# Attention values in fp32 matmuls, means moved between engines, and expert rows fetched by plain loads

## The chip, the cores and the metric

The kernel runs on one NeuronCore of a Trainium2 chip. The metric is the device time of one execution in microseconds (us). A core has five engines that work side by side, each through its own queue of instructions: PE (TensorE, the matrix unit; its weight loads are listed as PEld), DVE (VectorE), ACT (ScalarE), POOL (GpSimd) and SP (SyncE, here only an issuer of DMA transfers). POOL issues DMAs too, above all the indirect ones, whose row addresses come from a table. PE writes its results to PSUM[...]; DVE and ACT read them from there. A loaded tile lies in SBUF, the large on-chip memory.

## The reference

For 8 batches of 8 heads (576 positions, head size 64) two attentions are added, and their sum goes through a mixture of 8 experts in which each row visits one expert:

```python
q_d = q.reshape(B, H, Sd, 4, D).mean(axis=3)      # likewise k_d, v_d: means of 4 rows
out_d = sm_attn(q_d, k_d, v_d)                    # softmax attention, 144 x 144
out_up = np.repeat(out_d, 4, axis=2)
mask = np.abs(pos[:, None] - pos[None, :]) < 4    # local band, 7 wide
out_local = softmax(where(mask, scale * q @ k.T, -1e9)) @ v
x = (out_up + out_local)                          # as [4608 rows, 512]

e_idx = argmax(x @ w_gate)                        # one of 8 experts for each row
eom = sigmoid(x @ w_output_gate)
for e in range(8):
    out[rows of e] = gate_w * eom[:, e] * (relu(x_e @ w1[e]) @ w2[e])   # 512 -> 1024 -> 512
```

## The kernel before

The attention is done in 32 units, each of two heads of one batch. A list of tasks with an engine, a planned cost and a priority is put in order when the program is built, and each engine runs its tasks in that order. One unit is this:

```python
def cast(u, i):      # POOL: q and k to fp16
def v_high(u):       # ACT: upper half of v in fp16 (v scaled by VS = 1024)
    nc.scalar.activation(d["vh"][:, :, 0:D], d["vf"], AF.Copy, scale=VS)
def v_low(u):        # DVE: the rest, v*VS - high, in fp16
    nc.vector.scalar_tensor_tensor(d["vl"], in0=d["vf"], scalar=VS, in1=d["vh"][:, :, 0:D], ...)
def turn(u):         # PE: q and k turned, and their means of four by a 0.25-matrix pm
    for i in range(2):
        for m in range(6):
            nc.tensor.matmul(tf[:, i, S // 2:S // 2 + SD], lhsT=t16[:, m, :], rhs=pm[:, m, :], ...)
        for m in range(6):
            nc.tensor.transpose(tf[...][:, 96 * m:96 * m + 96], t16[:, m, :], id16[0:96, 0:96])
def turned(u):       # ACT: both out of PSUM (qkT: 1152 columns, qkd: 288 columns)
def v_means(u):      # PE: means of v's four rows, out of the two halves
    for w in range(NW):                                        # NW = 10 windows of rows
        for i, m in enumerate((d["vh"], d["vl"])):
            for h in range(2):
                nc.tensor.matmul(pd[:, h, c:c + D], lhsT=pv[r, w, :], rhs=m[r, w, 0:D], ...)
def vd_high(u):      # ACT
def vd_low(u):       # DVE
def scores(u):       # PE
    for g in range(2):                                         # the band's mask, 504 columns
        nc.tensor.matmul(ps[:, g, 0:NH], lhsT=id16, rhs=mk[:, g, :], ...)
    for h, r in hs:                                            # means: 128 of 144 keys
        mm(ps[:, h, 0:SD], kd[r, 0:128], qd[r])
    ...                                                        # 20 of 64x57 or 64x60: the band
    ...                                                        # means: the last 16 keys
def e_high(u):       # ACT: exp twice, once to fp16 and once in place in fp32
    nc.scalar.activation(d["eh"], ps, AF.Exp, scale=scale)
    nc.scalar.activation(ps, ps, AF.Exp, scale=scale)
def e_low(u):        # DVE: the rest in fp16
def values(u):       # PE: (high, high), (high, low), (low, high) for each product
    ...              # 60 + 12 + 12 matmuls of 64 or 65 columns
def norm(u):         # DVE: reciprocal of the sums, two products
```

After each fourth unit a batch's 5 tiles of 128 rows are finished (`upsample`, `x_sum`, `x_high`, `x_low`, `x_turn`, `logits`), gated in groups (`pick`, `ranks`, `gate_sums`, `rows`), and written row by row to a table in HBM with one region for each expert (`scatter`, 40 indirect DMAs). Then come the experts, 5 tiles of 128 rows each; for the first two experts 3 tiles are done early, when only six batches are in the table.

```python
def gather(e, j):    # POOL, 40 times: 128 rows of expert e by an index table
    nc.gpsimd.indirect_dma_start(out=ex[e]["xg"][:, j, :], in_=xs_dram.ap(),
        in_offset=bass.IndirectOffsetOnAxis(ap=posg[...][:, e, j:j + 1], axis=0), ...)
def rows_out(e, js): # DVE: the output rows; slots past the expert's count get a row out of bounds
    nc.vector.tensor_tensor(o[...], d["xg"][..., Dm // 2 + 1], none_i[i][...], op=ALU.add)
def g_turn(e, js):   # PE transposes; g_turned: DVE copies them out
def up(e, part, fs): # PE: 4 x 8 matmuls of 384 and of 256 columns against w1
def relu(...)        # ACT and DVE
def down(e, ...):    # PE: 8 matmuls of 512 columns for each tile against w2
def weigh(e, j):     # ACT: times the row's weight
def put(e, j):       # POOL, 40 times: 128 rows to the output by index
```

The weights of an expert come by four DMAs that POOL issues (`load_part`); there is room for three experts' weights at a time.

Of the kernel before, what the change touches and what calls it, by code (L numbers as in the profile page):

```python
# [19 lines left out]
KW = [57 * w - 1 for w in range(10)]  # L20
NW = 10
NB = 5
# [13 lines left out]
def kernel(  # L36
# [22 lines left out]
    VS = 1024.0  # L59
    GS = 1024.0  # L60
    XS = 4.0 * VS
# [13 lines left out]
    NH = SD + NL + NK  # L75
    LC = [SD + Q0[w] - NL * (w // 5) for w in range(NW)]
    TC = SD + NL
    mk = cst.tile([128, 2, NH], F16)
    nc.vector.memset(mk, 32.0)
    band = cst.tile([64, 2, 64], F16)  # L80
    pv = cst.tile([128, NW, 128], F16)
    nc.vector.memset(pv, 0.0)
    pb = cst.tile([64, NW, 17], F16)
# [5 lines left out]
    def make_band():  # L89


        nc.gpsimd.memset(band, 32.0)
        select(band, 4, [[0, 2], [1, 64]], -1, -8192.0)
        select(band, 2, [[0, 2], [-1, 64]], 1, -8192.0)
        select(band[:, 0], -1, [[0, 64]], 1, -8192.0)

    def make_mask(h):
        r = slice(64 * h, 64 * h + 64)
        copy = nc.scalar.copy if h else nc.vector.tensor_copy
        for g in range(2):  # L100
            x = band[:, 1, 3:60]
            c = SD + 60 * (1 - g)
            copy(mk[r, g, c:c + 228].rearrange("p (w c) -> p w c", w=4), _ap(x, [x.ap[0], [0, 4], x.ap[1]]))
        copy(mk[r, 0, SD:SD + 60], band[:, 0, 0:60])
        copy(mk[r, 1, SD + 228:SD + 288], band[:, 1, 3:63])

    def make_means():
# [3 lines left out]
        select(pb[:, 0:NW - 1], -1, [[1, NW - 1], [-4, 17]], 1)  # L111
        select(pb[:, 0:NW - 1], 4, [[-1, NW - 1], [4, 17]], -1)
        select(pb[:, 0:NW - 1], 60, [[0, NW - 1], [0, 17]], -1)
        select(pb[:, 1:NW - 1], -4, [[0, NW - 2], [0, 17]], 1)
        select(pb[:, NW - 1], 0, [[-4, 17]], 1)
        select(pb[:, NW - 1], 3, [[4, 17]], -1)

    def spread_means(h):
        r = slice(64 * h, 64 * h + 64)
        copy = nc.scalar.copy if h else nc.vector.tensor_copy  # L120
        x = pv[r, 0, 0:17]
        copy(_ap(x, [x.ap[0], [142, NW - 2], x.ap[1]]), pb[:, 0:NW - 2])
        copy(pv[r, NW - 2, 112:128], pb[:, NW - 2, 0:16])
        for c in (0, 32):
            copy(pv[r, NW - 1, c:c + 16], pb[:, NW - 1, 0:16])

    pm = cst.tile([96, 6, SD], F16)

    def make_pm():

        nc.gpsimd.memset(pm, 0.25)
        select(pm, 0, [[1, 6], [-4, SD]], 6)
        select(pm, 3, [[-1, 6], [4, SD]], -6)
# [22 lines left out]
    slot_i = cst.tile([128, E, CAPJ], I32)  # L156
    slot_f = cst.tile([128, E, CAPJ], F32)
    reg_i = cst.tile([128, E, CAPJ], I32)
    reg_f = cst.tile([128, E, CAPJ], F32)
# [3 lines left out]
    def make_gate():  # L163
# [14 lines left out]

        nc.gpsimd.iota(slot_i, pattern=[[0, E], [128, CAPJ]], base=0, channel_multiplier=1)
        nc.gpsimd.iota(reg_i, pattern=[[-REG, E], [128, CAPJ]], base=E * REG, channel_multiplier=1)  # L180
# [8 lines left out]
    def gate_consts():  # L189
        for x in w9_s:  # L190
            nc.vector.tensor_copy(x[:, :, E], past)
        for o, x in ((rev, rev_i), (slot_f, slot_i), (reg_f, reg_i)):
            nc.vector.tensor_copy(o, x)
# [5 lines left out]
    vh_s, vdh_s, xh_s = [], [], []  # L199
    for i in range(4):  # L200
        t_vh = cst.tile([128, NW, 66], F16, tag=f"vh{i}")
        nc.vector.memset(t_vh[:, :, 64:66], 0.25)
        vh_s.append(t_vh)
        t_vd = cst.tile([128, 2, 2, 66], F16, tag=f"vd{i}")
        nc.vector.memset(t_vd[:, :, :, 64:66], 0.25)
        vdh_s.append(t_vd)
# [3 lines left out]
    nc.vector.memset(cum, 0.0)  # L210

    posg = [cst.tile([128, E, CAPJ], I32, tag=f"posg{i}", name=f"posg{i}") for i in range(2)]
    none_i = [cst.tile([128, E, CAPJ], I32, tag=f"none{i}", name=f"none{i}") for i in range(2)]
    cnts = [cst.tile([128, E], F32, tag=f"cnts{i}", name=f"cnts{i}") for i in range(2)]
# [38 lines left out]
    def load_v(u):  # L253
        b, hp = u // NP, u % NP
        st.setdefault(u, {})["vf"] = vf = sbA.tile([128, NW, D], F32, tag="vf", name="vf", bufs=4)
        for h in range(2):
            s, r = v[b, 2 * hp + h], slice(64 * h, 64 * h + 64)
            if u == 0 and h == 0:

                nc.vector.memset(vf[0:1, 0, :], 0.0)  # L260
                nc.sync.dma_start(vf[1:64, 0, :], s[0:63, :])
                nc.sync.dma_start(vf[r, 1:NW, :], _ap(s, [[D, 64], [57 * D, NW - 1], [1, D]], KW[1] * D))
            else:
                nc.sync.dma_start(vf[r], _ap(s, [[D, 64], [57 * D, NW], [1, D]], -D))
# [5 lines left out]

    def v_high(u):
        d = st[u]
        d["vh"] = vh_s[u % 4]
        nc.scalar.activation(d["vh"][:, :, 0:D], d["vf"], AF.Copy, scale=VS)  # L274

    def v_low(u):
        d = st[u]
        d["vl"] = sbA.tile([128, NW, D], F16, tag="vl", name="vl", bufs=4)
        nc.vector.scalar_tensor_tensor(d["vl"], in0=d["vf"], scalar=VS, in1=d["vh"][:, :, 0:D],  # L279
                                       op0=ALU.mult, op1=ALU.subtract)  # L280

    def turn(u):
# [3 lines left out]
        for i in range(2):  # L286
            t16 = d["s16", i].rearrange("p m h d -> p m (h d)")
            for m in range(6):
                nc.tensor.matmul(tf[:, i, S // 2:S // 2 + SD], lhsT=t16[:, m, :], rhs=pm[:, m, :],  # L289
                                 start=(m == 0), stop=(m == 5), skip_group_check=True)  # L290
            for m in range(6):
                nc.tensor.transpose(tf[:, i, :].bitcast(F16)[:, 96 * m:96 * m + 96], t16[:, m, :], id16[0:96, 0:96])  # L292

    def turned(u):

        d = st[u]
        d["qkT"] = sbA.tile([128, 2 * S], F16, tag="qkT", name="qkT", bufs=3)
# [658 lines left out]
```

The softmax here doesn't subtract the row's maximum and nothing guards it: scores larger than these inputs give would overflow.

## Time and profile before

| | before |
|---|---|
| median of 3 runs | 520.38 us (519.46 to 521.83) |
| span of the profiled run | 519.3 us |
| PE busy | 415.0 us, 80% |
| DVE busy | 247.3 us, 48% |
| ACT busy | 244.6 us, 47% |
| POOL busy | 280.7 us, 54% |
| HBM read and written | 68.23 MB and 15.77 MB |

Busy time of an engine is the time in which at least one of its instructions ran. Matmuls run in a pipeline, so their records overlap, and a mean of 200 ns for a small matmul does not say that each takes 200 ns of PE: the distance between two starts does. The page cuts the span into 40 equal slices and gives each engine's busy share in tenths. A group line gives the program line, the engine, the operation, the tile written and those read, the shape, the count, then busy time and mean duration, and then the idle time of the engine just ahead of these instructions and what ended it. In a table of windows each row is a stretch of the span with the busy time of each engine, the clock granted to PE as a share of full speed, and the busy share of the DMA engines. The attention's matmuls end at 299 us of the span, the experts' first matmul starts at 323 us, and the last one ends at about 505 us.

### The profile page before, as it was taken

The page shows a single profiled execution, that of the slowest core. Times are in us where ns is not written, and L with a number is a line of the kernel's source. Part 1 is how long each engine was busy: PE and PEld are TensorE (multiplying, and loading weights), DVE is VectorE, ACT ScalarE, POOL GpSimd, SP SyncE. Part 2 cuts the span into 40 slices and gives each one's busy share as a digit, 9 for nine tenths or more (in the row PEclk, how much of TensorE's full clock was granted, in tenths as well). Part 3 has the DMA queues.
Part 4 walks back from the last instruction along what each step waited for, and adds up shares of the span by engine and source line. Part 5 has one row for each costly group of instructions (what it writes and reads, how often), then busy time and mean ns, then how long its engine had stood idle before and what let it go on. Part 6 is the DMA issues. An engine that isn't in the chain of part 4 may idle for free.

```text
span 519.3 us, 17157 instructions
## 1 busy us (share of the span) xinstructions
PE 415.0 (80%) x7567; PEld 291.3 (56%) x7567; DVE 247.3 (48%) x494; ACT 244.6 (47%) x403; POOL 280.7 (54%) x315
## 2 busy tenths in 40 slices
PE   4866996979978869899969566977689759889990
PEld 3645684666756757675946434535455435456540
DVE  5436975656757747756658474412232012322200
ACT  4646784557747557766647332312223232333340
POOL 8724754525866815948426545576786524572231
PEclk9878898588979797976889755998989899999996
DMA  9999649465455595461450101233579994594121
GB/s 193 216 190 204 148 112 166 123 114 114 132 155 145 131 214 131 136 156 47 70 97 31 57 20 50 69 120 103 127 159 212 208 218 96 138 193 120 62 92 39
DMA packets 76285, 66.34 MB, mean 128 GB/s; under 512 B 46962, under 2 KB 67507, under 8 KB 76200
## 3 DMA queue, kind: packets, MB, share of 16 engines
q0 software_dynamic: 19840, 35.74, 30.7%
q1 hardware_dynamic: 56360, 29.40, 26.2%
q8 instruction: 61, 1.00, 0.8%
q14 instruction: 24, 0.20, 0.1%
HBM read 68.23 MB, written 15.77 MB: 162 GB/s over the span
## 4 chain that ended last, share of the span: by engine, by line
PE 58%; issue 17%; DVE 7%; DMA 6%; POOL 5%; another core or an unknown queue 2%; ACT 2%; POOLq 0%; DVEq 0%
PE pu L636 8%; PE tqk L289 7%; PE ps L336 5%; PE us L430 5%; PE pd L313 5%; PE po L385 4%; PE py L659 4%; PE tqk L292 4%; PE ps L338 3%; PE po L391 3%; DMA w1sb<-in_moe_w_dram 3%; PE tp L445 2%; PE po L401 2%; PE lg L465 2%
## 5 line engine op out<-in xcount | busy, mean ns | idle before, releaser
L269 POOL CAST qk<-qk 96x768 f16<-96x768 f32 x64 | 55.7, 882 | 76.6 <-issue 35.1
L636 PE MATMUL pu<-xgT,w1sb 128*128 128x384 f16 (+1 forms) x512 | 80.2, 315 | 19.2 <-DVE xgT L619 9.5
L636 PEld LDWEIGHTS <-w1sb 128*128 128x128 f16 x512 | 52.4, 103 | 46.0 <-issue 25.0
L671 POOL DMA_INDIRECT out_dram<-y,oi x40 | 40.3, 1006 | 49.7 <-ACT y L667 42.0
L659 PE MATMUL py<-w2sb,hs 128*128 128x512 f16 x272 | 61.6, 379 | 0.0
L667 ACT ACTIVATE y<-py,xh 128x512 f32<-128x512 f32 x40 | 25.6, 684 | 74.3 <-PE py L659 34.8
L651 DVE TENSOR_SCALAR hs<-pu 128x256 f16<-128x256 f32 x56 | 23.3, 423 | 67.1 <-ACT hs L649 40.4
L289 PE MATMUL tqk<-pm,qk 96*128 96x144 f16 x384 | 44.7, 264 | 13.1 <-POOL qk L269 6.2
L551 POOL DMA_INDIRECT hx_xs<-xh,pos x40 | 41.7, 1043 | 19.7 <-issue 8.4
L440 POOL TENSOR_TENSOR t_xl<-xo,xh 128x512 f16<-128x512 f32 x38 | 45.6, 1215 | 10.6 <-ACT xh L437 10.2
L587 POOL DMA_INDIRECT xh<-hx_xs,posg x40 | 40.7, 1017 | 17.8 <-issue 10.5
L300 ACT COPY qkT<-tqk 128x1152 f16<-128x1152 f16 x32 | 35.8, 1118 | 22.4 <-PE tqk L292 22.4
L649 ACT ACTIVATE hs<-pu 128x384 f16<-128x384 f32 (+1 forms) x56 | 26.1, 475 | 42.7 <-PE pu L636 34.4
L289 PEld LDWEIGHTS <-qk 96*128 96x128 f16 x384 | 31.7, 115 | 18.6 <-issue 7.4
L659 PEld LDWEIGHTS <-hs 128*128 128x128 f16 x272 | 26.2, 98 | 28.4
L279 DVE SCALAR_TENSOR_TENSOR vl<-vf,t_vh 128x640 f16<-128x640 f32 x32 | 39.9, 1249 | 3.0 <-ACT t_vh L274 3.0
L360 DVE TENSOR_TENSOR el<-ps,eh 128x1008 f16<-128x1008 f32 x32 | 38.3, 1198 | 4.3 <-ACT ps L355 4.3
L354 ACT ACTIVATE eh<-ps 128x1008 f16<-128x1008 f32 x32 | 32.5, 1016 | 13.1 <-PE ps L336 12.6
L313 PE MATMUL pd<-vl,pv 64*128 64x64 f16 x640 | 29.1, 200 | 11.8 <-issue 11.7
L413 DVE TENSOR_TENSOR xo<-po,rs 128x448 f32<-128x448 f32 x64 | 37.0, 619 | 1.5
L292 PE MATMUL tqk<-id,qk 96*128 96x96 f16 x384 | 34.2, 236 | 4.0 <-issue 4.0
L423 POOL TENSOR_TENSOR xdl<-xo,xdh 72x512 f16<-72x512 f32 x15 | 18.9, 1273 | 33.1 <-ACT xdh L418 33.1
(144 smaller groups left out, 896.4 us busy)
## 6 DMA issues: line engine op xcount, KB each, us to landing
vf<-in_v_dram SPq DMA_DIRECT2D x63, 160.0 KB, 7.6
qk<-in_q_dram SPq DMA_DIRECT2D x32, 288.0 KB
qk<-in_k_dram SPq DMA_DIRECT2D x32, 288.0 KB, 4.6
w1sb<-in_moe_w_dram POOLq DMA_DIRECT2D x16, 512.0 KB
w2sb<-in_moe_w_dram POOLq DMA_DIRECT2D x16, 512.0 KB
hx_xs<-xh,pos POOLq DMA_INDIRECT x40
xh<-hx_xs,posg POOLq DMA_INDIRECT x40
out_dram<-y,oi POOLq DMA_INDIRECT x40
```

Source lines behind the costliest of these rows:

```text
L269: nc.gpsimd.tensor_copy(t16.rearrange("p m h d -> p h m d"), d["f", i])
L279: nc.vector.scalar_tensor_tensor(d["vl"], in0=d["vf"], scalar=VS, in1=d["vh"][:, :, 0:D], op0=ALU.mult, op1=ALU.subtract)
L289: nc.tensor.matmul(tf[:, i, S // 2:S // 2 + SD], lhsT=t16[:, m, :], rhs=pm[:, m, :], start=(m == 0), stop=(m == 5), skip_group_check=True)
L292: nc.tensor.transpose(tf[:, i, :].bitcast(F16)[:, 96 * m:96 * m + 96], t16[:, m, :], id16[0:96, 0:96])
L313: nc.tensor.matmul(pd[:, h, c:c + D], lhsT=pv[r, w, :], rhs=m[r, w, 0:D], start=(w == 0 and i == 0), stop=(w >= NW - 2 and i == 1), skip_g ...
L360: nc.vector.tensor_tensor(d["el"], d["ps"][:, :, 0:NH], d["eh"], op=ALU.subtract)
L440: (nc.vector if b == B - 1 and t % 2 else nc.gpsimd).tensor_tensor(t_xl[:, t], xo_s[b][:, t, :], xh_s[b % 4][:, t, 0:Dm], op=ALU.subtract)
L551: ins = nc.gpsimd.indirect_dma_start(out=xs_dram.ap(), out_offset=bass.IndirectOffsetOnAxis(ap=gs[n]["pos"][:, c:c + 1], axis=0), in_=xh_s ...
L587: nc.gpsimd.indirect_dma_start(out=ex[e]["xg"][:, j, :], out_offset=None, in_=xs_dram.ap(), in_offset=bass.IndirectOffsetOnAxis(ap=posg[0 ...
L636: nc.tensor.matmul(ps[:, i, 0:x.shape[2]], lhsT=wts[e][0][:, c, 128 * f:128 * f + 128], rhs=x[:, c, :], start=(c == 0), stop=(c == 3))
L659: nc.tensor.matmul(ps[:, i, :], lhsT=d["hs"][:, f, c:c + 128], rhs=wts[e][1][:, f, :], start=(f == 0), stop=(f == NG - 1))
L671: ins = nc.gpsimd.indirect_dma_start(out=out, out_offset=bass.IndirectOffsetOnAxis(ap=d["oj", j], axis=0), in_=d.pop(("y", j)), in_offset= ...
```

## The change

It does three things, and orders the tasks anew.

1. **No halves.** v and the exponentials stay in fp32, and each product of the values is one fp32 matmul. The steps that made the halves go. The ones' column that gives the sums is 1/4096 in v's tile.
2. **Means.** v's means are fp32 matmuls with 32 weight columns that write 32 rows of PSUM each; the means of q and k (as sums of four; the exponential's scale is divided by 16) are a reduction on DVE over the turned q and k, and no longer matmuls. The keys' means are scored in four pieces of 32 rows, and the mask covers only the band's 288 columns.
3. **Plain loads.** The first 640 rows of each expert's region are filled ahead with empty rows whose output row is out of bounds. The experts' rows then come by one plain load for a pass (10 in all, issued by SP), the index tables and the correction of output rows go, and `put` takes its rows straight out of what was loaded.

```diff
-    def v_high(u): ...
-    def v_low(u): ...
     def turn(u):
...
-                nc.tensor.matmul(tf[:, i, S // 2:S // 2 + SD], lhsT=t16[:, m, :], rhs=pm[:, m, :],
-                                 start=(m == 0), stop=(m == 5), skip_group_check=True)
-            for m in range(6):
                 nc.tensor.transpose(tf[:, i, :].bitcast(F16)[:, 96 * m:96 * m + 96], t16[:, m, :], id16[0:96, 0:96])
...
+    def qk_means(u):
+        nc.vector.tensor_reduce(d["qkd"], d["qkT"].rearrange("x (n r) -> x n r", r=4), axis=AX.X, op=ALU.add)
...
     def v_means(u):
         for w in range(NW):
-            c = D * (w == NW - 1)
-            for i, m in enumerate((d["vh"], d["vl"])):
-                for h in range(2):
-                    nc.tensor.matmul(pd[:, h, c:c + D], lhsT=pv[r, w, :], rhs=m[r, w, 0:D], ...)
+            for h in range(2):
+                j, c = (w // 2, 0) if w < 8 else (2 * h + 1, D)
+                nc.tensor.matmul(pd[32 * j:32 * j + 32, h, c:c + D], lhsT=pv[64 * h:64 * h + 64, w, :],
+                                 rhs=d["v"][64 * h:64 * h + 64, w, 0:D], start=(w % 2 == 0), stop=(w % 2 == 1), ...)
-    def vd_high(u): ...
-    def vd_low(u): ...
+    def vd_out(u):                                  # ACT: three copies out of PSUM
...
     def scores(u):
-            nc.tensor.matmul(ps[:, g, 0:NH], lhsT=id16, rhs=mk[:, g, :], ...)
-        for h, r in hs:
-            mm(ps[:, h, 0:SD], kd[r, 0:128], qd[r])
+            nc.tensor.matmul(ps[:, g, 0:NL], lhsT=id16, rhs=mk[:, g, :], ...)
+        for j in range(4):
+            for h, r in hs:
+                mm(ps[32 * j:32 * j + 32, h, MC:NH], kd[r, MW[2 * j]:MW[2 * j] + 32], qd[r])
...
-        nc.scalar.activation(d["eh"], ps, AF.Exp, scale=scale)
-        nc.scalar.activation(ps, ps, AF.Exp, scale=scale)
-    def e_low(u): ...
+        d["e"] = e = sbA.tile([128, 2, NH], F32, tag="e", name="e")
+        nc.scalar.activation(e[:, :, TC:NH], d["ps"][:, :, TC:NH], AF.Exp, scale=scale / 16.0)
+        nc.scalar.activation(e[:, :, 0:TC], d["ps"][:, :, 0:TC], AF.Exp, scale=scale)
     def values(u):                                  # 20 + 4 + 4 fp32 matmuls of 65 columns
+                    nc.tensor.matmul(po[h][64 * a:64 * a + 64, t, :], lhsT=e[r, w // 5, LC[w]:LC[w] + 64],
+                                     rhs=t_v[r, w, 0:65], start=(t == 0), stop=False, skip_group_check=True)
...
     def norm(u):                                    # DVE: two reciprocals and three products, the means' rows apart
...
+    def prefill(e):                                 # SP, 8 times
+        nc.sync.dma_start(xs_dram.ap()[r:r + 128 * CAPJ, :].rearrange("(p j) d -> p (j d)", p=128), ...)
-    def gather(e, j): ...
-    def rows_out(e, js): ...
+    def fetch(e, part):                             # SP, 10 times
+        nc.sync.dma_start(ex[e]["xg"][:, j0:j1, :].rearrange("p j d -> p (j d)"),
+                          xs_dram.ap()[r:r + 128 * (j1 - j0), :].rearrange("(p j) d -> p (j d)", p=128))
...
-    LEAN = {"band": 0.1, "cast": -1.2, "eh": -2.15, ...}       # shifts of the tasks' priorities
+    LEAN = {"ahead": 67.55, "band": -52.05, "cast": -27.9, ...}
...
-                task(("scat", x, t), "POOL", 1.35, ..., [("rows", b)], scatter, n, x, t, ...)
+                task(("scat", x, t), "POOL", 1.35, ..., [("rows", b)] + [("fill", e) for e in range(E)], scatter, n, x, t, ...)
```

## The prediction

> **What bounds the kernel now.** I read the slices first, then a table of windows, then the chain that ended last, then groups and the timelines of single engines.
>
> ```profile
> PE   4866996979978869899969566977689759889990
> PEclk9878898588979797976889755998989899999996
> DMA  9999649465455595461450101233579994594121
> PE 58%; issue 17%; DVE 7%; DMA 6%; POOL 5%; another core or an unknown queue 2%; ACT 2%; POOLq 0%; DVEq 0%
> ```
>
> A slice is 13 us. PE is the fullest engine in nearly every slice and holds 58% of the chain; no other engine has over 7%. DMA is full only at the start and around the experts' weights. The windows split the span into three stages:
>
> ```profile
> 100.00:200.00 100.00, 83.90 (x2219) 66.79 (x2216) 64.01 (x115) 60.79 (x96) 53.25 (x54) 0.84 0.64 143
> 200.00:290.00 90.00, 79.25 (x2157) 60.62 (x2156) 60.33 (x110) 57.81 (x89) 54.59 (x55) 0.87 0.40 91
> 290.00:320.00 30.00, 17.03 (x244) 11.72 (x244) 15.09 (x43) 8.52 (x16) 13.06 (x13) 0.54 0.13 42
> 320.00:353.00 33.00, 26.23 (x174) 14.15 (x172) 12.16 (x40) 7.09 (x16) 20.57 (x21) 0.91 0.27 87
> 353.00:400.00 47.00, 39.48 (x269) 25.76 (x269) 12.78 (x32) 14.16 (x30) 34.37 (x36) 0.93 0.68 153
> ```
>
> The columns are PE, PEld, DVE, ACT, POOL, clock, DMA share, GB/s. In the attention (to 299 us) PE is busy 84 to 88%, DVE and ACT about 64%, so PE bounds it, with short waits between. From 290 to 353 us, the last batches' gating and the table's last rows, PE is busy 43 of 63 us. Then the experts: in 353 to 519 us I add the windows to 132 us of PE in 166. The holes in PE there have names in PE's timeline and in the waits:
>
> ```profile
> 353.40 5.32 PE L636 MATMUL pu<-xgT,w1sb 128*128 128x256 f16 x32 [4.01 <-DVE xgT L619]
> 377.40 7.11 PE L636 MATMUL pu<-xgT,w1sb 128*128 128x256 f16 x39 [4.02 <-DVE xgT L619]
> 420.05 0.61 PE L608 MATMUL gtp<-id,xh 128*128 128x128 f16 x8 [3.64 <-DVE xgT L619]
> DVE oi L599 <- DMA out_dram<-y,oi: 23.6, 5, 7.3
> ```
>
> PE waits for turned rows (xgT), and DVE, which turns them out, stands behind the correction of output rows (oi), which waits for an earlier output transfer. All holes over 0.2 us from 353 to 466 us add up to 24 us.
>
> **What the skill says.** The Trainium skill's page "FP8 and Floating Point Precision", section TensorE Precision Notes, says that a true fp32 product is four passes through the array. The kernel before has no fp32 matmul, so no trace here shows it yet. "TensorEngine Tiling (Array Packing)", Key Properties, says that tiles work independently, weight loads included. The trace agrees for fp16: in the timeline at 126 us four 64x64 matmuls of 65 columns take one step, and the next four start 30 to 40 ns later. "VectorE: DVE Perf Modes", section on the perf-mode tier table, gives a reduction no faster mode for 16-bit data; the trace has only short reductions (264 ns for 80 fp16 elements), which can't tell. "TensorE: Matmul & The Clock Gate", Part 1, says an idle PE falls to half its clock. The trace agrees: at 119.8 us such steps are 55 ns apart, and the window with most idle PE has a clock of 0.54.
>
> **The change part by part.** In 100 to 200 us there are 132 mean matmuls of line 289, 12 for a unit: 11 units, so a unit takes 9.1 us and 7.6 us of PE.
>
> ```profile
> L289 PE MATMUL tqk<-pm,qk 96*128 96x144 f16 x384 | 44.7, 264 | 13.1 <-POOL qk L269 6.2 <-DVE xo L413 3.9 <-issue 3.0
> L279 DVE SCALAR_TENSOR_TENSOR vl<-vf,t_vh 128x640 f16<-128x640 f32 x32 | 39.9, 1249 | 3.0 <-ACT t_vh L274 3.0
> L360 DVE TENSOR_TENSOR el<-ps,eh 128x1008 f16<-128x1008 f32 x32 | 38.3, 1198 | 4.3 <-ACT ps L355 4.3
> L354 ACT ACTIVATE eh<-ps 128x1008 f16<-128x1008 f32 x32 | 32.5, 1016 | 13.1 <-PE ps L336 12.6 <-PE us L430 0.5
> L587 POOL DMA_INDIRECT xh<-hx_xs,posg x40 | 40.7, 1017 | 17.8 <-issue 10.5 <-DMA hx_xs<-xh,pos 2.4 <-DVE xh L547 2.4
> ```
>
> PE, one unit at full clock. A column costs 0.42 ns (16 output matmuls of 512 columns in 3.62 us, the last one's 0.38 taken off: 0.216 us each).
> - Means of q and k: in the timeline six matmuls of 144 columns span 0.55 us, one of them 0.23, so 0.065 us a step; 12 of them: -0.78.
> - Mask: 504 to 288 columns, twice: 432 x 0.42 ns = -0.18.
> - Keys' means in 8 pieces instead of 2, partly side by side: +0.1.
> - Values: before, 84 matmuls from 125.85 to 127.97 us less a hole of 0.47: 1.65 us. After, with four passes of 65 x 0.42 = 27 ns: five rounds of four tiles side by side 0.55; four full-width ones 0.44; two pairs 0.22; 0.2 for the pipeline's end: 1.4. Weight loads that don't hide add perhaps 0.2: counted as 1.6, so -0.05.
> - v's means: 0.77 us before (the chain has 0.76 at 133 us); after, 10 pairs x 4 x 27 ns = 1.08 if the column tiles don't overlap, about half if they do. Counted 0.9: +0.13.
>
> Sum -0.78, and over the clock of 0.84, -0.9 us of 7.6. If PE stays 84% busy, a unit takes 8.0 instead of 9.1 us, 34 us in 32 units. I count 26, because a new step now stands in each unit's path (DVE's reduction of 1152 elements; by DVE's 1198 ns for 1008, some 1.35 us) and because more idle PE may lower the clock.
>
> ACT, one unit: gone are 0.74 + 0.41 + 2 x 1.02 + 0.37 = 3.55 us; the rows of 256 and 1008 elements give 0.85 ns an element and about 0.16 us fixed, so the new exponentials (432 and 576) cost 1.17 and the three copies 0.7: -1.7 us. DVE: gone are 1.25 + 1.20 + 0.42 = 2.87; the reduction costs 1.35, the longer norm 0.3: -1.2 us. Both lie beside PE; they shorten the time that a unit's scores hold PSUM (two exponentials and a subtraction, 3.2 us, become 1.2) and so fill some of PE's short holes.
>
> POOL: 40 gathers of 1.02 us and 0.3 between go, 53 us of its queue. Six stand between the last rows' steps (306 to 332 us), and five from 344.4 to 350.7 us ahead of the 4.0 us hole at 353. One load replaces each set: I count -8 us for 300 to 353 us. In the expert stage, of the 24 us of holes those that end on xgT or come from oi should mostly go, those that wait for weights should not: -13 us.
>
> SP: 8 fills of 128 x 5160 bytes, 5.3 MB; at the 200 GB/s of the page's fullest slices some 26 us of DMA time. In the built program they come behind the loads of the first ten units, where DMA is about half busy: 0.
>
> Sum: 26 + 8 + 13 = 47, so 520.4 - 47 = 473; I say 474 us.
>
> **The rivals.** (1) fp32 matmuls don't run side by side, or load their weights in the open. Then 48 of them at 108 ns are 5.2 us where I count 2.5, 2.7 us more in each unit, 86 us in all: 474 + 86 = 560. Against it: fp16 tiles, which load weights just as often, do overlap; for it: nothing in the trace has fp32. (2) DVE's reduction or DMA takes PE's place. DVE would be 51 of 100 us, ACT 43, so no engine is near; but with fills DMA rises from 187 us of the first 290 (shares of the windows times their lengths) to some 213 of 265. Then the attention gains only 10 us: about 490. (3) The experts are held by weights: the five last experts' 21 MB need 105 us at 200 GB/s, and the slices at 390 to 430 us already show 208 to 218. Then 13 becomes 5: about 482. (4) All holes in PE close: the attention gains 34 and the rest 30: about 455.
>
> **Range and chances.** Rivals 2 and 3 together give about 500, rival 4 455; 450 to 505 should hold it 8 times in 10. Three separate gains would all have to fail, or rival 1 come true, for it to be slower, which I give 0.07; faster by over 2% gets 0.86, between them 0.07.
>
> **What would show it.** Right: no line of means in `turn`; values' and v's means' fp32 groups spanning about 1.6 and 0.9 us a unit; attention's last matmul near 270 us; ACT and DVE under 210 us busy each; no hole of 4 us ahead of the experts' first full passes; PE's busy share at or above 80%. Wrong: fp32 groups spanning over 2.5 us together at full clock beyond these, a clock under 0.8 in the attention, PE waiting on qkd or on v's load, or holes ended by w1sb transfers.

## The result and the profile after

| | before | after |
|---|---|---|
| median, runs of both side by side | 521.04 us (519.46 to 521.83) | 450.65 us (449.35 to 456.48) |
| ratio | | 0.864, 95% interval 0.861 to 0.868 |
| span of the profiled run | 519.3 us | 448.3 us |
| start of the attention's last matmul (values) | 299.1 us | 259.6 us |
| first expert matmul (`up`) | 323.4 us | 284.8 us |
| first full pass of an expert | 353.4 us | 311.9 us |
| last `down` matmul | 505.2 us | 436.7 us |
| HBM written | 15.77 MB | 21.05 MB |

The change takes 70 us off, where 46 were predicted. 450.65 us is at the very bottom of the range of 450 to 505.

The page of the changed kernel: engines, slices (11.2 us each now) and the chain by engine.

```profile
PE 389.8 (87%) x6479; PEld 273.3 (61%) x6479; DVE 203.9 (45%) x478; ACT 200.6 (45%) x400; POOL 227.8 (51%) x278
...
PE   3887988988978989889879978797999999999990
...
PEclk9959669899597999878955576899999999999996
DMA  9999979796562796993281013117799999781121
...
PE 74%; issue 12%; ACT 3%; POOL 3%; DVE 3%; DMA 2%; another core or an unknown queue 1%; POOLq 0%; ACTq 0%; DVEq 0%
```

PE's share of the chain has grown from 58 to 74%, and from about 314 us on, in the experts' full passes, its digits are nines, at full clock. Cut at the four points of the table above, the windows say where the 71 us of span went. First before, then after (columns: stretch, length, busy time of PE, PEld, DVE, ACT and POOL, clock, DMA share, GB/s):

```profile
20.00:299.10 279.10, 232.38 (x6190) 179.63 (x6189) 177.21 (x304) 170.15 (x261) 154.21 (x172) 0.83 0.60 129
299.10:323.40 24.30, 15.13 (x176) 9.98 (x173) 15.29 (x40) 7.23 (x14) 12.10 (x12) 0.50 0.11 34
323.40:505.20 181.80, 155.87 (x992) 92.11 (x988) 45.00 (x125) 54.78 (x105) 97.94 (x102) 0.96 0.59 136
```

```profile
20.00:259.60 239.60, 212.38 (x5047) 163.72 (x5032) 134.16 (x296) 125.59 (x260) 135.80 (x163) 0.80 0.73 167
259.60:284.80 25.20, 17.38 (x231) 11.81 (x228) 16.42 (x43) 8.84 (x18) 16.60 (x16) 0.72 0.23 80
284.80:436.70 151.90, 148.60 (x981) 89.54 (x979) 43.01 (x105) 55.07 (x104) 59.36 (x64) 0.99 0.70 163
```

The attention is 39.5 us shorter, the stretch between attention and experts 0.9 us longer, the experts 29.9 us shorter, the tail 2.5 us. Two figures can be had from each row. The length less PE's busy time is PE's idle time. Busy time by the clock is roughly PE's *work*, what it would take at full clock (the clock has two digits, so such a figure is good to 2 or 3 us). In the attention, idle fell from 46.7 to 27.2 us, and work from 193 to 170. In the experts, idle fell from 25.9 to 3.3 us; the work stayed (150 and 147).

The new instructions, in PE's timeline of the changed kernel between 100 and 130 us, with the lines of other tiles left out:

```profile
105.22 0.74 PE L304 MATMUL pd<-t_v,pv 64*32 64x64 f32 x40
...
126.04 0.81 PE L359 MATMUL po<-t_v,e 64*64 64x65 f32 x40 [0.45 <-ACT vd L314]
126.78 0.73 PE L363 MATMUL po<-vd,e 128*72 128x65 f32 x8
127.45 0.47 PE L368 MATMUL po<-vd,e 32*72 32x65 f32 x8
```

An fp32 matmul leaves two records: `values` has 28 in the program and 56 here. At full clock a unit's values run from 126.04 to 127.92, so 1.88 us, and its v means take 0.74 us.

### The profile page after: what moved, and what is told of

It is laid out like the page before. It is cut to its first block, busy times and chain, and to the rows that moved or that the text cites. A ratio compares the mean times of both kernels' runs of the same rounds, so it can differ in the third digit from the quotient of the medians.

```text
span 448.3 us, 14930 instructions
## 1 busy us (share of the span) xinstructions
PE 389.8 (87%) x6479; PEld 273.3 (61%) x6479; DVE 203.9 (45%) x478; ACT 200.6 (45%) x400; POOL 227.8 (51%) x278
## 3 DMA queue, kind: packets, MB, share of 16 engines
HBM read 68.23 MB, written 21.05 MB: 199 GB/s over the span
## 4 chain that ended last, share of the span: by engine, by line
PE 74%; issue 12%; ACT 3%; POOL 3%; DVE 3%; DMA 2%; another core or an unknown queue 1%; POOLq 0%; ACTq 0%; DVEq 0%
PE pu L593 13%; PE py L616 10%; PE po L359 7%; PE us L402 6%; PE pd L304 6%; PE po L363 6%; PE ps L324 6%; PE tqk L282 4%; PE po L368 3%; PE tp L417 3%; PE lg L437 3%; PE ps L326 3%; PE tp L419 2%; DMA out_dram<-y,xh 2%; PE gtp L565 2%
## 5 line engine op out<-in xcount | busy, mean ns | idle before, releaser
L628 POOL DMA_INDIRECT out_dram<-y,xh x40 | 40.1, 1002 | 54.6 <-ACT y L624 48.2
L412 POOL TENSOR_TENSOR t_xl<-xo,xh 128x512 f16<-128x512 f32 x38 | 43.9, 1169 | 31.6 <-ACT xh L409 28.2
L295 DVE TENSOR_REDUCE qkd<-qkT 128x288 f16<-128x1152 f16 x32 | 42.7, 1344 | 15.0 <-ACT qkT L288 14.9
L304 PE MATMUL pd<-t_v,pv 64*32 64x64 f32 x1280 | 32.5, 256 | 10.9 <-issue 10.0
L359 PE MATMUL po<-t_v,e 64*64 64x65 f32 x1280 | 34.4, 257 | 8.0 <-issue 6.0
L343 ACT ACTIVATE e<-ps 128x432 f32<-128x432 f32 x32 | 17.1, 533 | 46.2 <-PE ps L324 21.7
L359 PEld LDWEIGHTS po<-t_v,e 64*64 64x64 f32 x1280 | 28.5, 164 | 14.5 <-issue 7.1
L406 DVE TENSOR_TENSOR xo<-us,xo 128x512 f32<-128x512 f32 x40 | 26.6, 685 | 19.5 <-PE us L402 16.8
L304 PEld LDWEIGHTS pd<-t_v,pv 64*32 64x32 f32 x1280 | 25.0, 126 | 16.8 <-issue 13.1
L282 PE MATMUL tqk<-id,qk 96*128 96x96 f16 x384 | 26.7, 226 | 8.0 <-POOL qk L273 6.1
L409 ACT CAST xh<-xo 128x512 f16<-128x512 f32 x40 | 24.3, 619 | 14.5 <-DVE xo L406 12.8
```

The lines of the kernel that those rows point to most:

```text
L295: nc.vector.tensor_reduce(d["qkd"], d["qkT"].rearrange("x (n r) -> x n r", r=4), axis=AX.X, op=ALU.add)
L304: nc.tensor.matmul(pd[32 * j:32 * j + 32, h, c:c + D], lhsT=pv[64 * h:64 * h + 64, w, :], rhs=d["v"][64 * h:64 * h + 64, w, 0:D], start=(w ...
L359: nc.tensor.matmul(po[h][64 * a:64 * a + 64, t, :], lhsT=e[r, w // 5, LC[w]:LC[w] + 64], rhs=t_v[r, w, 0:65], start=(t == 0), stop=False, ...
L412: (nc.vector if b == B - 1 and t % 2 else nc.gpsimd).tensor_tensor(t_xl[:, t], xo_s[b][:, t, :], xh_s[b % 4][:, t, 0:Dm], op=ALU.subtract)
L628: ins = nc.gpsimd.indirect_dma_start(out=out, out_offset=bass.IndirectOffsetOnAxis(ap=d["xg"][:, j, Dm // 2 + 1:Dm // 2 + 2], axis=0), in_ ...
```

## The experiments

The three parts of the change can be taken apart. The tables below give PE's work and idle time in the attention (20 us to the last values), and the expert stage (first `up` to last `down`). Executions of one kernel fell into a faster and a slower state; times and ratios here are of the faster one, while the traces of e8, e11 and e12 are of slower executions, so that their work and idle times are only roughly comparable. Chips differ as well: beside the first set of runs (e1 to e4) the kernel before took 499.4 to 502.9 us, beside the second (e5 to e8) it scattered from 489.8 to 516.6 us, which makes those intervals wide, and beside the third (e9 to e12) it took 520.8 to 525.3 us. So times are compared as ratios to it, and stages by their traces. Where a ratio is given without an interval, or none is given, there were too few comparable runs.

### Each part alone

**e1_loads_only** is the kernel before with part 3 alone (fills, plain loads, `put` from the loaded rows).

```diff
-    def gather(e, j): ...   # and rows_out, index tables
+    def prefill(e): ...     # SP, 8 times
+    def fetch(e, part): ... # SP, 10 times
```

> The kernel before with part 3 alone: filled regions and plain loads in place of the gathers, with the old priorities, and the attention untouched. Theory that each part pays in its own stage: the attention still ends near 299 us, the experts (from their first matmul to the end, 196 us before, 164 us in the changed kernel) take about 165 us, the whole about 490 us. Rival, that the new order of tasks closed the experts' holes: the experts stay at 185 to 196 us, the whole at 510 to 521 us.

**e2_attention_only** is parts 1 and 2 alone; the 40 gathers stay.

```diff
-    def v_high / v_low / vd_high / vd_low / e_low, turn's pm matmuls
+    def qk_means, vd_out, fp32 v_means and values
```

> The changed kernel with the gathers kept (no fills, index tables and corrected output rows as before) and the old priorities: parts 1 and 2 alone. Theory that each part pays in its own stage: the attention ends near 262 us, the experts still take about 195 us, the whole about 483 us. Rival, that the new order gave much of the attention's 40 us: it ends at 275 us or later, the whole at 497 us or more.

**e3_old_order** is the whole change with the task shifts of the kernel before.

```diff
-    LEAN = {"ahead": 67.55, "band": -52.05, ...}
+    LEAN = {"band": 0.1, "cast": -1.2, ...}
```

> The changed kernel with all three parts and the old priorities. Theory that the parts pay and the new order is a small thing: 450 to 458 us, and the gains of the two runs with one half each add up to this one's. Rival, that the new order carries it: 475 us or more, with holes before the experts' matmuls or an attention that ends after 270 us.

Measured (e1 to e3 on one chip; the rows "before" and "after" are the profiles shown above, from another):

| | time, ratio to before | attention: work, idle, clock, end | experts |
|---|---|---|---|
| before | 1 | 193, 46.7 us, 0.83, 299.1 us | 181.8 us |
| e1, loads only | 461.30 and 467.67 us, 0.927 (0.917 to 0.937) | 191, 41.3 us, 0.87, 280.9 us | 150.5 us |
| e2, attention only | 461.02 us, 0.920 | 170, 28.8 us, 0.88, 241.8 us | 177.8 us |
| e3, old order | 446.97 and 447.48 us, 0.892 (0.887 to 0.897) | 170, 25.3 us, 0.78, 263.1 us | 148.1 us |
| after | 450.24 us, 0.864 (0.861 to 0.868) | 170, 27.2 us, 0.80, 259.6 us | 151.9 us |

In PE's work and idle time the parts add up. The experts are short wherever the loads are plain (148 to 152 us) and long wherever they are gathers (178 to 182 us), whatever the attention does. The attention's work and most of its idle time go only with parts 1 and 2.

e3's expectation was that the times would add up too; they do not. Against a kernel before of about 501 us, e1 is faster by about 37 us and e2 by about 40, but e3, which has both, by about 54 and not 77. The difference lies in the attention: e3 has the same work as e2 and less idle time, and ends it 21 us later, at a clock of 0.78 instead of 0.88. The attention rows, e2 first:

```profile
20.00:241.80 221.80, 193.04 (x5042) 152.64 (x5039) 137.20 (x304) 125.62 (x262) 140.16 (x167) 0.88 0.77 160
```

```profile
20.00:263.10 243.10, 217.78 (x5121) 167.57 (x5103) 141.48 (x307) 127.23 (x265) 141.72 (x169) 0.78 0.73 168
```

The fills alone don't do it: e1, with fills and the old attention, ends it at 280.9 us, and e4 (below), without fills on the same chip, at 279.5 us, both at 0.87. The last section says more of the clock. The 299.1 us that e1 was expected to keep belong to another chip.

The new order isn't needed for any of the figures of work and idle time. The ratio of e3 is worse than that of the change (0.864, and 0.855 on a third chip, e9), but they come from different chips, and what the order is worth is not settled better than that. The expert rows of e1 and of e2 side by side:

```profile
303.90:454.40 150.50, 148.18 (x992) 89.92 (x988) 43.30 (x107) 55.26 (x105) 57.98 (x63) 1.00 0.68 162
```

```profile
267.50:445.30 177.80, 157.49 (x993) 92.80 (x990) 44.40 (x125) 55.35 (x105) 97.69 (x102) 0.94 0.60 139
```

With plain loads PE is idle for 2.3 of 150 us and POOL is busy for 58 us, not 98.

### Why the experts gain 30 us

**e4_oi_room** takes away only the wait that the profile before named, oi, by room for more of these tiles.

```diff
-        ... sbA.tile([128, CAPJ], I32, tag="oi", name="oi", bufs=4)
+        ... sbA.tile([128, CAPJ], I32, tag="oi", name="oi", bufs=10)
```

> The kernel before with ten tiles instead of four for the corrected output rows, so that DVE's correction no longer waits for an old output transfer (23.6 us of waits in five places). Theory that this wait in DVE's queue makes the experts' holes: 8 us or more faster, about 508 us. Rival, that the gathers' turn in POOL's queue makes them: within 3 us of 521 us, the holes of 4 us stay and now end on the gathers.

Measured: 489.73 and 492.16 us, 0.979 (0.973 to 0.986); the expert stage is 169.0 us, 13 us less than in the kernel before and 9 less than in e2, which has the gathers and oi and ran on e4's chip. So oi was worth 9 to 13 us. PE's timeline of e4 shows what then comes last:

```profile
349.85 0.51 PE L608 MATMUL gtp<-id,xh 128*128 128x128 f16 x4 [2.58 <-DMA xh<-hx_xs,posg]
...
396.51 3.89 PE L636 MATMUL pu<-xgT,w1sb 128*128 128x384 f16 x14 [8.83 <-ACT y L667]
```

PE waits for a gather's landing, and once 8.83 us for ACT's y, which itself waited 10.0 us for room: an output transfer landed 15.4 us after its issue.

**e5_pool_loads** is the e3 kernel with plain loads, but 40 of them in POOL's queue, in the gathers' places.

```diff
-        nc.sync.dma_start(ex[e]["xg"][:, j0:j1, :] ...)         # 10 on SP
+        nc.gpsimd.dma_start(ex[e]["xg"][:, j, :], ...)          # 40 on POOL
```

> The changed kernel with the old priorities, and its plain loads issued by POOL, one for each tile of 128 rows (40), so that they stand in POOL's queue where the gathers stood; the output rows are still taken straight from what was loaded. Theory that the gathers' place in POOL's queue made the larger share of the experts' holes (18 of 31 us; the wait on corrected rows the other 13): from the first to the last expert matmul 160 us or more, against 148 with SP's loads and 182 in the kernel before. Rival, that being indirect and needing the corrected rows was the cause: 152 us or less.

Measured: 455.19 and 455.48 us. The expert stage is 155.1 us, between the two expectations and neither of them: 3 to 7 us above the three kernels with loads on SP (148.1 to 151.9).

```profile
284.10:439.20 155.10, 149.60 (x992) 90.19 (x988) 43.31 (x107) 55.11 (x105) 79.34 (x101) 0.99 0.69 162
```

If these shares add up, then of some 30 us (27.3 from e2 to e1, 33.7 from before to e3) 9 to 13 hung on the output rows' correction (oi) and 3 to 7 on the places in POOL's queue, and the rest went with the gathers themselves. The queue's share may well be larger: five of e5's loads hold POOL for 2.8 us, five gathers for 6.3 us, so e5 put back less than half of the time for which gathers hold the queue. How far the rest is that time, their landing or the order they force was not separated, and e4's stage holds the 8.83 us wait, which may be its own. What a pass waited for shows in POOL's timeline of the kernel before, just ahead of the hole at 353 us:

```profile
344.37 1.05 POOL L587 DMA_INDIRECT xh<-hx_xs,posg  x1 [0.30 <-issue]
...
349.65 1.00 POOL L587 DMA_INDIRECT xh<-hx_xs,posg  x1 [0.31 <-issue]
...
362.63 1.00 POOL L587 DMA_INDIRECT xh<-hx_xs,posg  x1 [0.30 <-issue]
363.64 0.79 POOL L227 DMA_DIRECT2D w1sb<-in_moe_w_dram  x1
...
373.89 0.99 POOL L587 DMA_INDIRECT xh<-hx_xs,posg  x1 [0.30 <-issue]
374.87 0.81 POOL L227 DMA_DIRECT2D w1sb<-in_moe_w_dram  x1
```

Five gathers 1.3 us apart hold a pass for 6 us of queue time, and the loads of weights stand behind them: two w1sb loads are issued 11 us apart. In the changed kernel POOL issues them as soon as `up` has freed the buffer:

```profile
315.87 1.51 POOL L231 DMA_DIRECT2D w1sb<-in_moe_w_dram  x2 [2.36 <-PE pu L593]
319.36 1.43 POOL L231 DMA_DIRECT2D w1sb<-in_moe_w_dram  x2 [1.99 <-PE pu L593]
```

### Which half of the attention's change pays

**e6_means_on_pe** is the changed kernel with the means of q and k as matmuls again and ACT's copy of them; DVE's reduction goes. v and the exponentials stay fp32.

```diff
+                nc.tensor.matmul(tf[:, i, S // 2:S // 2 + SD], lhsT=t16[:, m, :], rhs=pm[:, m, :], ...)
+        nc.scalar.copy(d["qkd"]..., d["t"][:, :, S // 2:S // 2 + SD])
-    def qk_means(u): ...
```

> The changed kernel with its own priorities and the means of q and k as matmuls again (12 of 144 columns a unit), copied out by ACT; no reduction on DVE. PE work of the attention is counted as busy time by granted clock, from 20 us to its last matmul: 191 us before, 170 in the changed kernel. Theory that this move alone makes the difference: PE work 190 to 194 us, the attention 20 us or more longer than in the changed kernel, the whole about 475 us or 0.91 to 0.92 of before. Rival, that the relief of ACT and DVE made the attention's gain: less than 10 us longer, about 0.88 of before.

**e10_dve_means_before** is the reverse: the kernel before, halves and gathers kept, with only q's and k's means moved to DVE (a reduction and a scaling by a quarter).

```diff
-                nc.tensor.matmul(tf[...], lhsT=t16[:, m, :], rhs=pm[:, m, :], ...)
+        nc.vector.tensor_reduce(d["qkd"], d["qkT"]..., axis=AX.X, op=ALU.add)
+        nc.vector.tensor_scalar_mul(d["qkd"], d["qkd"], 0.25)
```

> The kernel before with only the means of q and k moved from PE to a reduction on DVE (and a short scaling there, since they are sums of four); halves, gathers and old priorities stay. Theory that the relief of ACT and DVE made the attention's gain and this move by itself is worth little: PE work falls from 191 to about 172 us, but PE's busy share falls from 84% to 80% or less as DVE becomes nearly full, and the ratio to before is 0.97 or more. Rival, that PE work sets the time: the share stays at 84%, the attention is 22 us shorter, the ratio 0.95 to 0.96.

Measured: e6 444.21 to 448.13 us, 0.886 (0.858 to 0.914). e10 546.62 and 549.30 us, 1.047 (1.040 to 1.054), so the move by itself makes the kernel slower. With before and after this is a square of four, by halves and by the place of the means:

| attention | means on PE | means on DVE |
|---|---|---|
| halves kept | before: work 193, idle 46.7, clock 0.83, ends at 299.1 us | e10: work 166, idle 66.6, clock 0.69, ends at 327.3 us |
| no halves | e6: work 188, idle 15.5, clock 0.84, ends at 259.6 us | after: work 170, idle 27.2, clock 0.80, ends at 259.6 us |

The rows of e10 and of e6:

```profile
20.00:327.30 307.30, 240.73 (x5879) 175.10 (x5880) 222.47 (x375) 163.89 (x235) 156.40 (x179) 0.69 0.59 120
```

```profile
20.00:259.60 239.60, 224.13 (x5423) 179.25 (x5423) 97.09 (x273) 133.04 (x289) 138.54 (x165) 0.84 0.76 168
```

Read across: the move of the means takes 18 to 27 us of work from PE, as predicted, and adds 12 to 20 us of idle time, at a lower clock. With the halves gone, what it gains it gives back; the attention ends at the same 259.6 us, and no difference between e6 and the change is resolved by their ratios. At one and the same clock of 0.84 the move would be worth 18 / 0.84 - 12 = 9 us, an estimate that no run showed as time. Read down: taking the halves away changes work by 5 us or less either way, and takes 31 to 39 us of idle time. The lower row has part 3 and the new order as well, but these don't explain it: e2 has neither, differs from e10 by part 1, the fp32 form of v's means and the new scores, and has 28.8 us of idle time where e10 has 66.6.

e10's attention is 28.2 us longer than that of the kernel before: 19.9 us of it are idle time, and 8.3 are busy time, because less work ran at a lower clock. DVE is busy for 72% of it, not nearly full as had been expected.

How far PE waited for the removed steps of ACT and DVE themselves, the traces tell only in part. Of PE's holes over 0.2 us in the attention, the profile names another engine at the end of 35 of 65 us in e10 and of 6 of 28 us in e2, but of only 11 of 45 us in the kernel before. There 34 us end on "issue", that is on nothing that the profile shows, against 23 us in the changed kernel and 15 in e6. The largest entry among PE's waits before (total, times, longest):

```profile
PE pd L313 <- issue: 15.8, 15, 3.4
```

So it is shown that the idle time goes with part 1 and the pieces tied to it. That it goes because ACT and DVE are relieved is named by the profile for e10, and argued for the rest. A rival stands untested: the same edit shortens PE's own stream from 7183 matmuls in e10's program to 4943 in e2's.

**e11_pe_means_dve_copy** is e6 with DVE in ACT's place for the copy of the means.

```diff
-        nc.scalar.copy(d["qkd"]..., ...)
+        nc.vector.tensor_copy(d["qkd"]..., ...)
```

> The changed kernel with the means of q and k as matmuls again, but copied out of PSUM by DVE (288 columns, 0.4 us) and not by ACT; its own priorities. Theory that the share of PE depends on how much ACT and DVE have in a unit's path: PE work 188 us, PE busy 93% or more of the attention, the whole within 2% of the changed kernel. Rival, that PE work sets the time: 18 us more work give 22 us more attention, the whole 4 to 5% above the changed kernel.

Measured: 475.29 us; PE's work is 192 and its idle time 28.9 us, at a clock of 0.78. This was meant to show that e6 didn't hang on who copies, and failed: it is slower by about 6% than the change beside it (445.34 and 449.33 us), nearer to the rival than to the theory, and PE is busy for 89% of the attention, where 93% were expected. DVE's waits in e11 show one place where it is held:

```profile
DVE qkd L306 <- ACT qkT L299: 35.2, 12, 6.2
```

In the built order DVE's copy stands behind ACT's copy of the turned q and k, and DVE's whole queue waits there, 35.2 us in 12 waits. The turned tile's room in PSUM, too, comes free only after that copy. So e6's result holds for its own queue order, and little work on ACT and DVE alone (both under 46% busy here) doesn't keep PE fed; how much of e11's loss is this wait and how much the lower clock is open.

**e12_two_adds** is the changed kernel with the reduction written as two fp16 additions.

```diff
-        nc.vector.tensor_reduce(d["qkd"], d["qkT"]..., axis=AX.X, op=ALU.add)
+        nc.vector.tensor_tensor(y, x[:, :, 0, :], x[:, :, 1, :], op=ALU.add)
+        nc.vector.tensor_tensor(d["qkd"], y[:, :, 0], y[:, :, 1], op=ALU.add)
```

> The changed kernel with the reduction of q's and k's means written as two fp16 additions, of 576 and of 288 results. Theory that the reduction's 1.34 us in each unit's path holds PE's share at 88%: the two take 0.9 us or less, the share rises to 90% or more, the whole 4 to 8 us under the changed kernel. Rival, that DVE has room and the path doesn't matter: within 3 us of it.

**e9_after_again** is the changed kernel as it is, beside e10, e11 and e12.

> The changed kernel itself beside the next three, so that they can be compared. Theory: PE work of the attention (busy time by granted clock, from 20 us to its last matmul) 170 us, PE busy 88 to 90% of that stretch, ratio to before 0.86 to 0.89. Rival, that the order of its tasks matters more than three per cent: well below the 0.89 of the same kernel with the old priorities.

Measured: e9 445.34 and 449.33 us, 0.855 (0.848 to 0.862), just under the 0.86 to 0.89 that the theory had, with work 172 us and PE busy for 88%; e12 453.24 to 459.16 us, 0.872 (0.865 to 0.879), so slightly slower, with idle 34.6 instead of 27.5 us. But the step did not get shorter. DVE's two groups in e12 (busy time and mean ns of one):

```profile
L297 DVE TENSOR_TENSOR qk<-qkT 128x576 f16<-128x576 f16 x32 | 27.2, 850 | 10.4 <-ACT qkT L288 9.8
L298 DVE TENSOR_TENSOR qkd<-qk 128x288 f16<-128x288 f16 x32 | 20.6, 645 | 1.2
```

Each addition takes 0.46 us in the median, as planned, but their means sum to 1.50 us, against 1.34 for the reduction: 19 of the 64 took over 0.5 us, up to 5.94, and each of these ran while POOL had an instruction running. The 32 reductions of the changed kernel take 1.336 to 1.354 us whatever POOL does. So e12 doesn't tell whether a shorter step would give the idle time back.

### What fp32 costs PE

**e7_upper_halves** is e3 with v's means and the values on the upper 16 bits of each operand, as bf16. It leaves the lower halves out of the computation; the instructions stay in their places.

```diff
+    hi = lambda x: x.bitcast(bfloat16)[:, :, 1::2]
-    matmul(po..., lhsT=e..., rhs=t_v...)
+    matmul(po..., lhsT=hi(e)..., rhs=hi(t_v)...)
```

> The changed kernel with the old priorities; the values' and v's means' matmuls read only the upper 16 bits of each fp32 operand (a bf16 view with a stride), one pass instead of fp32. It leaves the lower halves out, so the output is less exact. It measures what fp32 costs. Theory that PE sets the pace of the attention and fp32 is four passes: values 0.8 and v's means 0.4 us a unit instead of 1.75 and 0.75, PE work 170 less 35 to 45 us, the whole 30 us or more under the same kernel in fp32. Rival, that another engine is close behind PE: PE work falls as much, the whole by less than 15 us.

**e8_wide_v_means** is e3 with the v means of the first 8 windows by 128 weight columns, mostly zeros, instead of 32.

```diff
-                    nc.tensor.matmul(pd[32 * j:32 * j + 32, h, c:c + D], lhsT=pv[64 * h:64 * h + 64, w, :], ...)
+                    nc.tensor.matmul(pd[:, h, 0:D], lhsT=pw[64 * h:64 * h + 64, w, :], ..., start=(w == 0), stop=(w == 7))
```

> The changed kernel with the old priorities; v's means of the first eight windows use 128 weight columns (zeros outside the 32 that count) and write all 128 rows, so neighbouring windows share their columns of the array and can't run side by side. Theory that the 32-row tiles overlap: v's means take 1.1 us a unit instead of 0.74 at full clock, PE work rises by 9 to 12 us, the whole by about 12 us. Rival, that rows of different windows never overlapped: within 3 us.

Measured: e7 405.03 to 409.57 us, 0.810 (0.795 to 0.825); e8 470.60 to 472.28 us, 0.936 (0.911 to 0.962). Their attention rows, e7 first:

```profile
20.00:218.20 198.20, 175.27 (x3604) 122.44 (x3603) 137.63 (x302) 125.73 (x259) 142.22 (x169) 0.78 0.93 205
```

```profile
20.00:297.00 277.00, 269.52 (x5182) 221.14 (x5183) 142.15 (x313) 128.96 (x266) 142.62 (x169) 0.85 0.63 148
```

Against e3 (work 170, idle 25.3, attention to 263.1 us, clock 0.78), e7 has work 137 and ends at 218.2 us: 33 us less work at the same clock is 42 us, and 45 came. So PE's work does set the pace once the halves are gone, and fp32 costs about 1.1 us of it in each unit. DMA is then 93% busy, with fills and all, and still hides.

In e8 the work is 229 us, 59 more than in e3, where 9 to 12 were expected, and PE is idle for 7.5 us only; the wider v means account for about 48 of the 59 (1.61 us in each of 30 units). PE's timeline of e8:

```profile
102.64 2.00 PE L308 MATMUL pd<-t_v,pw 64*128 64x64 f32 x32
104.58 0.41 PE L313 MATMUL pd<-t_v,pv 64*32 64x64 f32 x8
```

These two lines are 2.35 us from start to end, against 0.74 for the same means in the changed kernel. The records of the wide ones start 0.056 us apart; two row groups run side by side, so 0.11 us a record in each. The Trainium skill, "TensorE: Matmul & The Clock Gate", section LDWEIGHTS (loading the stationary operand), has a load's time as its columns over 1.2, in ns, which makes an estimate of 107 ns for 128 columns. That fits, and so do the values' full-width matmuls of 72 columns: an estimate of 60 ns by the page, 65 ns from one record to the next in the changed kernel's trace. It does not fit e7's bf16 matmuls with the same 72 columns, which follow each other after 39 ns; there the measurement decides. And the wide form also gives up the column tiles, which may have run side by side, and e8 doesn't separate the two.

## Why the prediction was right, and where its sizes were wrong

The direction and all the stages that it named were right; the sum of -47 was short by 24 us of span. By its own stretches:

| stretch | predicted | measured |
|---|---|---|
| attention | -26 us | -39.5 us |
| to the first full pass (299.1 to 353.4, now 259.6 to 311.9 us) | -8 us | -2.0 us |
| from there to the last `down` matmul (151.8, now 124.8 us) | -13 us | -27.0 us |
| tail | 0 | -2.5 us |

**PE, one unit: right in sum.** It had -0.78 us at full clock, which over 30 units is 23 us; the work fell by 193 - 170 = 23. Inside the sum two errors partly cancel, which was luck: the values take 1.88 us instead of 1.6, and a full-width fp32 matmul in them about 0.13 us instead of 0.108 (its two records are 65 ns apart); v's means take 0.74 us instead of 0.9: in each of their two row groups the records, two for a matmul and not four, follow each other after 27 ns. Whether their column tiles overlap does not show. Together the two make 2.62 us, where the prediction had 2.5. That answers rival 1: fp32 tiles run side by side, and "560" is out. The four passes from which the prediction reckoned can't be counted in the trace, which has two records for a matmul; e7's bf16 full-width matmuls are 39 ns apart, so fp32 was 3.3 times as dear here.

**"If PE stays 84% busy ... I count 26": the step that failed.** The prediction took the work as the gain and took 8 us off for DVE's new step and the clock. What the runs show is two things of opposite sign. The move of the means does cost idle time (12 to 20 us in the square above), so the reason for the deduction was right and its size too small. But the removal of the halves, for which the prediction had "so fill some of PE's short holes" and no number, is worth 31 to 39 us of idle time, more than anything else in the attention. Net of the two, PE's idle time fell by 19.5 us, half of the attention's 39.5, and PE's share rose from 83.3 to 88.6%. e10 is the clearest sign: less work for PE, with the halves still on ACT and DVE, is slower by 5%, though part of that is its lower clock.

**ACT and DVE: right in size, wrong in use.** Their groups in the changed kernel (busy time and mean ns of one):

```profile
L295 DVE TENSOR_REDUCE qkd<-qkT 128x288 f16<-128x1152 f16 x32 | 42.7, 1344 | 15.0 <-ACT qkT L288 14.9
...
L343 ACT ACTIVATE e<-ps 128x432 f32<-128x432 f32 x32 | 17.1, 533 | 46.2 <-PE ps L324 21.7
```

The reduction takes 1344 ns where 1.35 us was predicted; so the trace now agrees with the Trainium skill, "VectorE: DVE Perf Modes", section on the perf-mode tier table, which gives a reduction no faster mode: 1152 fp16 elements at 1.17 ns each, against 1.19 for the fp32 row that the 1.35 came from. ACT's first exponential takes 0.53 us and both together 1.18, where 1.17 was predicted. Both engines ended below 210 us of busy time. They were on no long stretch of the chain before (ACT 2%, DVE 7%), and still most of the idle time went with the halves; the share of the chain didn't tell it.

**"-8 us for 300 to 353 us": failed.** 2 us came. The 4.0 us hole at 353 went (0.34 us in front of the first full pass now), but the gating ahead of it grew by 0.9 us, and PE now waits 2.44 us for ACT's hsA in the early passes. The six gathers between the last rows' steps were not what that stretch waited for: in e1, without any gather, attention and experts are 23.0 us apart instead of 24.3.

**"those that wait for weights should not: -13 us": failed the good way.** 27 us came. The prediction left about half of the 24 us of holes to waits for weights, but the profile of the kernel before ends none of PE's waits from 353 to 505 us on a load of weights: 14.4 us end on xgT, 6.7 on DVE's hs, 2.1 on ACT's y. These all closed. That weight loads behind gathers had a part in it, as POOL's timelines above suggest, is not shown. The clock of the stage also rose from 0.96 to 0.99, worth 155.87 - 148.60 = 7 us of busy time. Rival 3 is out: 163 GB/s over the stage was enough.

**Fills: 0, right as far as is shown.** 5.3 MB more is written and DMA's share in the attention rose from 0.60 to 0.73. With the old attention fills cost 1.4 us (e1 against e4). With the new one, work and idle time are no larger with fills (e3) than without (e2); that e3's clock is lower is not explained. Rival 4, about 455 us, came nearest in number; it was held to be the edge and not the centre. Its mechanism, all holes in PE closed, came true in the experts (3.3 us left) but not in the attention, where 27.2 us stay.

**The signs that it named.** Those for "right" came, most of them further than said: attention's end at 259.6 us instead of 270, PE's share at 87%, no hole of 4 us ahead of the first full passes. Of those for "wrong", only the clock came near, 0.80 in the attention, and it was below 0.8 in e3.

## What to carry to other kernels

Split a stage's time into PE's work (busy by clock) and its idle time, and predict each by itself: here the predicted work was right and half the attention's gain was idle time that had no number. Steps removed from engines that are about 60% busy went with more gain here than the work removed from the one that is 84% busy, and work moved onto such an engine made the kernel slower in e10. Where rows are gathered by index tile by tile, a layout that one plain load can read frees the issuing queue for the loads behind it as well.

## What the runs showed of the hardware that was not expected

- An fp32 matmul shows as two weight loads and two matmuls. With 128 weight columns in place of 32 the v means took 2.35 us instead of 0.74 in a unit, and the kernel's ratio went from 0.892 to 0.936.
- Fp16 additions on DVE took 0.46 us in the median and up to 5.94 us while POOL was working (e12); the reduction kept to 1.336 to 1.354 us.
- The mean clock of the attention was between 0.69 and 0.88 in different runs and kernels, with the same attention code at 0.78 (e3), 0.80 (after) and 0.88 (e2). It doesn't follow the share of idle time: e1 had 0.87 with 16% idle, e11 0.78 with 10%.
- It follows how the idle time is bunched. In every trace the clock is either 1 or 0.5, and changes only in steps of 3.4 us. In the changed kernel's attention, from 15 us on, 42 such steps ran at 1: the 10 after which the clock fell had PE idle for 29% (1.0 us) or more, the other 32 for 24% or less. It came back only after steps in which PE was idle for 4% or less. So PE's hole of 2.31 us at 43.1 us is followed by a fall at 45.4 us that lasts 6.8 us. In the kernel before the line is less sharp: 12 falls after 36% or more, and no fall in 44 steps with up to 41%. By the same count e2's attention fell 7 times and had 16 steps at half clock, e3's 9 times and 31, with less idle time. Why e3's holes fell so is open.
